# Attention, low-rank mixing and a feed-forward on one core: the feed-forward of batches 2 to 7 in tiles of 384 tokens instead of 288

## The chip, the core and the metric

The kernel runs on one NeuronCore of a Trainium2 chip. TensorE (PE) multiplies matrices into PSUM; VectorE (DVE), ScalarE (ACT) and GpSimd (POOL) do the element-wise work; SyncE (SP) issues the transfers. Each engine takes its instructions strictly in the order in which they were written into its queue. The metric is the device time of one execution in microseconds (us); lower is better. Differences under about 0.2% (2 us) are within what a measurement of this kernel can tell from no change.

## The reference

Eight batches, eight heads, 576 positions, 64 numbers per head. For each batch the kernel computes attention, mixes it over the positions with a matrix of rank 32, and puts a feed-forward of width 2048 behind it:

```python
q_d, k_d, v_d = means over groups of 4 positions          # 144 positions
out_up   = repeat(softmax(q_d k_d^T / 8) v_d, 4)           # coarse attention
out_local = softmax(masked q k^T / 8, |i - j| < 4) v       # local attention, 7 keys
x  = (out_up + out_local), heads side by side              # [576, 512] for a batch
u  = x + (x^T U V)^T                                       # U: 576x32, V: 32x576
out = u + relu(u w1) w2                                    # w1: 512x2048, w2: 2048x512
```

Everything is float32. The kernel splits each operand of the large products into a high and a low part and sums three products (high by high, high by low, low by high), so that TensorE's one-pass form of float32 keeps the accuracy.

## The kernel before

**Feed-forward.** The 4608 tokens (8 batches of 576) are cut into 16 tiles of 288, two for each batch. For a tile, `u` lies transposed in SBUF as `uH` and `uL`, four blocks of 128 channels each. The hidden width of 2048 is cut into 16 chunks of 128. A step is one tile and one chunk: `ffn1` (line 893) makes the chunk of the hidden layer in one PSUM bank with 12 matmuls (4 channel blocks by 3 products), ACT writes its relu as `hH`, DVE the rest as `hL`; three steps later `ffn2` (line 915) adds the chunk's part of the output to four PSUM banks with 12 matmuls (4 output blocks by 3 products). Each of these matmuls has 128 weight columns of its own and 288 moving columns, and each is preceded by its weight load. After the 16th chunk POOL adds `uH` and `uL` into an output buffer `o1`, DVE adds the PSUM bank, and SP stores it. There are 256 steps, 6144 matmuls.

**Attention.** The eight heads of a batch are done as four pairs. Pairs 0 to 3 (batch 0) take an early path at the start. The other 28, called late pairs here, go through this chain: scores on PE (lines 745 and 758), softmax of the coarse attention, its product with `v` (line 564), a store to memory (`up_s`, line 573) and a load in another layout (`ul`, line 817); the local attention in five pieces, in which POOL multiplies (`Pt`, line 829) and DVE sums (line 834); a store (`x_s`, line 836) and two loads, `xL` with positions across partitions (line 852) and `Y` in blocks of 32 (line 863). DVE transposes `Y` into `xT` (line 868); ACT rounds `xL` into `xH` (line 869), POOL takes the difference (line 870), PE multiplies both with `U` (line 878, "hu"), the result goes into `stk`, and PE multiplies it with `V` (line 715, "u"). DVE adds `xT`, and ACT and POOL write the pair's block of `uH` and `uL` for both tiles of the batch (lines 719 to 724). A tile's first step needs all four blocks.

**Buffers.** `uH` and `uL` have room for two tiles: the one in work and the next. `xT` has four places, one for each pair of a batch. `xL`, `xH` and `Y` have one place each, `Pt` three.

**What sets the order.** Nothing runs when it is defined. Every operation goes into a plan with a duration, a latency, a priority and the buffers it uses; `Plan.run` (line 94) plays the plan through on five model engines and then emits the instructions in the order of the start times that it found. On the chip this order is fixed for each engine. Attention operations of pair p have priorities of 10 p and a little more, feed-forward matmuls 1000 and more: a feed-forward step fills PE wherever no attention operation is ready in the model. `dma` (line 261) gives a transfer its model latency, with an addition `late` that grows with the priority.

Of the kernel before, what the change touches and what calls it, by code (L numbers as in the profile page):

```python
# [200 lines left out]
def attn_mix_ffn_kernel(ctx: ExitStack, tc, q, kp, vp, qT, kT, v, U, Ub, V, w1, w2, edge, band, eye, pool, vw, ident, outT):  # L201
# [507 lines left out]
    def u_tail(b, hp, stk, lt, xT, bank, prio):  # L709
        for t in range(NT):  # L710
            tsl = slice(t * TN, (t + 1) * TN)
            pu = bank("ps_u", 1 - t)

            def um(tsl=tsl, pu=pu):
                nc.tensor.matmul(pu()[:, :TN], lt(), Vst[:, tsl], start=True, stop=True)  # L715
# [6 lines left out]
            act(TN, lambda uH=uH, uf=uf: nc.scalar.activation(uH()[:, hp, :], uf(), AF.Copy),  # L722
                [ufk], [(uH, hp)], prio, 0.1)
            pool_tt(TN, lambda uH=uH, uL=uL, uf=uf: nc.gpsimd.tensor_tensor(  # L724
                out=uL()[:, hp, :], in0=uf(), in1=uH()[:, hp, :].bitcast(F32), op=ALU.subtract),
                [ufk, (uH, hp)], [(uL, hp)], prio)
# [114 lines left out]
    def u_of(b, t):
        if (b, t) not in u_bufs:
            u_bufs[(b, t)] = (buf(ffn, [128, NDC, TN], F32R, "uH", bufs=2), buf(ffn, [128, NDC, TN], F32R, "uL", bufs=2))
        return u_bufs[(b, t)]
# [211 lines left out]
```

## Time and profile before

| what | value |
|---|---|
| median of 3 runs | 1018.7 us (1018.46 to 1018.81) |
| profiled execution, its own time | 1018.72 us |
| span of that execution, first to last instruction | 1016.9 us, so 1.8 us lie outside it |
| mean granted TensorE clock | 0.991 of full speed |
| PE busy | 981.1 us (96%) |
| POOL, DVE, ACT busy | 578.6, 471.1, 387.5 us (57%, 46%, 38%) |
| mean busy share of the 16 DMA engines (kernel's own queue) | 46.2% |

A row that groups instructions gives the line of the kernel, the engine, the operation, what is written and read, the shapes and the count, then the time in which at least one of them ran, the mean of one in ns, the engine's idle time just before them, and what ended it. Matmuls overlap: one is shown as about 297 ns long, while the next starts after less than half of that, so for PE the distance from start to start tells more than the duration. In a table of windows the number behind an engine's busy time is the count of instructions that touch the window, and PEclk is the granted clock as a share of full speed.

### The profile page before, as it was taken

How to read it: one execution, taken by the hardware profiler on the slowest of the kernel's cores; microseconds unless marked ns; L12 is line 12 of the kernel's file. 1: busy time of each engine (PE TensorE's matmuls, PEld its weight loads, DVE VectorE, ACT ScalarE, POOL GpSimd, SP SyncE). 2: the span in 40 equal slices, each digit the busy share in tenths (PEclk: the TensorE clock that was granted, in tenths of full speed). 3: DMA queues.
4: the chain of work that ended last, by engine and by line, in shares of the span. 5: the costliest groups of instructions: out<-in, count | busy, mean ns of one | idle time of the engine just before them, and what ended most of it. 6: DMA issues, size and time to landing. Idle time of an engine off the chain costs nothing.

```text
span 1016.9 us, 26970 instructions
## 1 busy us (share of the span) xinstructions
PE 981.1 (96%) x10820; PEld 962.4 (95%) x10820; DVE 471.1 (46%) x945; ACT 387.5 (38%) x1239; POOL 578.6 (57%) x651
## 2 busy tenths in 40 slices
PE   5889899999999999999999999999999999999998
PEld 4679789989999999999999999999999999999998
DVE  5788864534544445454443445445443344221111
ACT  4866644433343342443443333333433232111110
POOL 6667897867565557675756657476675543211010
PEclk9979999999999999999999999999999999999999
DMA  9677955646364465564455553446555241000000
GB/s 262 196 233 210 278 132 125 169 100 148 81 148 106 120 134 138 119 142 106 106 144 123 139 122 92 114 101 159 132 130 122 65 99 53 8 6 19 6 20 24
DMA packets 222981, 120.23 MB, mean 118 GB/s; under 512 B 174772, under 2 KB 199176, under 8 KB 222856
## 3 DMA queue, kind: packets, MB, share of 16 engines
q1 hardware_dynamic: 222856, 118.51, 46.2%
q8 instruction: 85, 1.39, 0.6%
q14 instruction: 40, 0.33, 0.1%
HBM read 87.60 MB, written 30.86 MB: 116 GB/s over the span
## 4 chain that ended last, share of the span: by engine, by line
PE 87%; DMA 3%; POOL 3%; ACT 3%; DVE 2%; issue 1%; SPq 1%; POOLq 0%; ACTq 0%; DVEq 0%
PE ps_h L902 37%; PE acc L926 37%; PE ps_a L564 3%; PE ps_b L745 2%; PE ps_hu L878 2%; PE ps_t L551 1%; DMA vr<-in_v 1%; PE ps_b L758 1%; DMA gT<-in_kT 1%; POOL Pt L829 1%; PE ps_u L715 1%; POOL W L357 1%; PE ps_a L499 1%; DMA wr<-in_W 0%; DMA xL<-x_s 0%
## 5 line engine op out<-in xcount | busy, mean ns | idle before, releaser
L926 PE MATMUL acc<-hH,W 128*128 128x288 f32 x2048 | 463.1, 299 | 3.0 <-POOL W L357 3.0
L902 PE MATMUL ps_h<-uH,W 128*128 128x288 f32 x2048 | 455.5, 297 | 6.3 <-DVE hL L911 5.9
L902 PEld LDWEIGHTS ps_h<-uH,W 128*128 128x128 f32 x2048 | 345.6, 189 | 8.3 <-DVE hL L911 7.4
L926 PEld LDWEIGHTS acc<-hH,W 128*128 128x128 f32 x2048 | 344.3, 188 | 5.1 <-POOL W L357 4.1
L902 PE MATMUL ps_h<-uL,W 128*128 128x288 f32 x1024 | 304.0, 297 | 2.2 <-POOL uL L724 2.2
L911 DVE SCALAR_TENSOR_TENSOR hL<-ps_h,hH 128x288 fp32r<-128x288 f32 x256 | 116.7, 456 | 400.6 <-ACT hH L910 400.0
L926 PE MATMUL acc<-hL,W 128*128 128x288 f32 x1024 | 301.2, 294 | 0.0
L829 POOL TENSOR_TENSOR Pt<-vl,at 128x896 f32<-128x896 f32 (+1 forms) x140 | 242.5, 1808 | 56.4 <-DVE acc L834 49.9
L910 ACT ACTIVATE hH<-ps_h 128x288 fp32r<-128x288 f32 x256 | 105.1, 410 | 440.2 <-PE ps_h L902 440.1
L902 PEld LDWEIGHTS ps_h<-uL,W 128*128 128x128 f32 x1024 | 193.9, 189 | 2.4 <-POOL uL L724 2.4
L926 PEld LDWEIGHTS acc<-hL,W 128*128 128x128 f32 x1024 | 192.9, 188 | 0.0
L834 DVE TENSOR_REDUCE acc<-Pt 128x128 f32<-128x1024 f32 (+1 forms) x140 | 150.9, 1104 | 9.4 <-POOL Pt L829 4.8
L870 POOL TENSOR_TENSOR xL<-xL,xH 116x640 fp32r<-116x640 f32 x28 | 44.0, 1571 | 91.5 <-ACT xH L869 82.0
L724 POOL TENSOR_TENSOR uL<-xT,uH 128x288 fp32r<-128x288 f32 x64 | 50.2, 808 | 70.2 <-ACT uH L722 70.1
L937 POOL TENSOR_TENSOR o<-uH,uL 128x288 f32<-128x288 f32 x64 | 49.7, 811 | 55.1 <-DMA out_t<-o 55.1
L776 ACT ACTIVATE se<-ps_b 96x114 f32<-96x114 f32 x112 | 40.0, 357 | 57.1 <-PE ps_b L751 35.6
L823 ACT ACTIVATE Pt<-ul 128x128 f32<-128x128 f32 (+1 forms) x140 | 49.8, 442 | 21.6 <-DVE acc L834 17.6
L522 POOL TENSOR_TENSOR vr<-vr 72x256 f32<-72x256 f32 x56 | 41.4, 740 | 23.7 <-DMA vr<-in_v 23.7
L357 POOL TENSOR_TENSOR W<-c,W 128x512 fp32r<-128x512 f32 x32 | 41.3, 1292 | 13.1 <-ACT W L354 12.8
L537 ACT ACTIVATE E<-ps_b,nb 72x144 f32<-72x144 f32 x112 | 40.9, 373 | 0.6
L532 DVE TENSOR_REDUCE mx<-ps_b 72x2 f32<-72x288 f32 x56 | 23.1, 448 | 35.4 <-ACT se L776 32.9
L940 DVE TENSOR_TENSOR o<-acc,o 128x288 f32<-128x288 f32 x64 | 26.6, 452 | 24.3 <-PE acc L926 21.9
(134 smaller groups left out, 894.6 us busy)
## 6 DMA issues: line engine op xcount, KB each, us to landing
wr<-in_W SPq DMA_DIRECT2D x32, 512.0 KB
vl<-in_vp SPq DMA_DIRECT2D x56, 240.0 KB
vr<-in_v SPq DMA_DIRECT2D x64, 144.0 KB
out_t<-o SPq DMA_DIRECT2D x64, 144.0 KB
gT<-in_kT SPq DMA_DIRECT2D x28, 291.0 KB
gq<-in_qT SPq DMA_DIRECT2D x28, 288.0 KB
up_s<-od SPq DMA_DIRECT2D x112, 72.0 KB
ul<-up_s SPq DMA_DIRECT2D x28, 288.0 KB
```

The source lines that it names most:

```text
L357: pool_tt(1.0 * n, lambda: nc.gpsimd.tensor_tensor(out=lo_out(), in0=ta()[l0:], in1=hi_out()[l0:].bitcast(F32), op=ALU.subtract), [t, *own ...
L522: pool_tt(256, lambda x=x: nc.gpsimd.tensor_tensor(out=x()[:, :, 0:2, :], in0=x()[:, :, 0:2, :], in1=x()[:, :, 2:4, :], op=ALU.add), [x], ...
L724: pool_tt(TN, lambda uH=uH, uL=uL, uf=uf: nc.gpsimd.tensor_tensor(out=uL()[:, hp, :], in0=uf(), in1=uH()[:, hp, :].bitcast(F32), op=ALU.su ...
L823: act(n * D, lambda n=n, ps=ps, Pt=Pt: nc.scalar.activation(Pt()[:, :n, :, 7], ul()[:, ps, :], AF.Copy), [ul], [(Pt, 1)], prio, 0.16)
L829: nc.gpsimd.tensor_tensor(out=Pt()[:, :n, :, 0:7].rearrange("p s d o -> p o s d"), in0=win, in1=at()[:, ps, :].rearrange("p s o -> p o s") ...
L834: dve(8.5 * n * D, lambda n=n, ps=ps, Pt=Pt: nc.vector.tensor_reduce(out=acc()[:, ps, :], in_=Pt()[:, :n], axis=AX.X, op=ALU.add), [(Pt, 0 ...
L870: pool_tt(640, lambda: nc.gpsimd.tensor_tensor(out=xL(), in0=xL().bitcast(F32), in1=xH().bitcast(F32), op=ALU.subtract), [xL, xH], [xL], prio)
L902: nc.tensor.matmul(ps()[:, :TN], W1[fc]()[:, w, dc, :], u()[:, dc, :], start=(n == 0), stop=(n == 3 * NDC - 1))
L910: last_h[i] = act(TN, lambda: nc.scalar.activation(hH(), ps()[:, :TN], AF.Relu), [ps], [hH], FIRST, 0.05)
L911: dve(TN, lambda: nc.vector.scalar_tensor_tensor(hL(), ps()[:, :TN], 0.0, hH().bitcast(F32), op0=ALU.max, op1=ALU.subtract), [ps, hH], [hL ...
L926: nc.tensor.matmul(ac[e]()[:, :TN], W2[fc]()[:, w, es], hx(), start=(fc == 0 and n == 0), stop=(fc == NFC - 1 and n == 2))
L937: pool_tt(TN, lambda e=e, o1=o1: nc.gpsimd.tensor_tensor(out=o1()[:, :TN], in0=uH()[:, e, :].bitcast(F32), in1=uL()[:, e, :].bitcast(F32), ...
```

## The change

- **Tiles.** Batches 0 and 1 keep their four tiles of 288 tokens. The 3456 tokens of batches 2 to 7 are cut into nine tiles of 384, across the borders of batches: of each three tiles the middle one holds 192 tokens of one batch and 192 of the next. A matmul of these tiles has 384 moving columns. There are 13 tiles, 208 steps and 4992 feed-forward matmuls, 3456 of them 384 wide.
- **The last product of a pair** ("u", now line 720) is cut at the borders of tiles: for batches 2 to 7 into 384 and 192 columns in place of 288 and 288.
- **Room.** The fourth channel block of the wide `uH` and `uL` lies in a place of its own (`u3`); `Y` and `xH` share one place; `Pt` has two places instead of three; the attention weights `at` are written over `ms`, which gets two places; the scratch of the weight conversion and the output buffers share one tile, cut into three and four.
- **The model behind the order.** A transfer's added latency falls from 1.5 or 2.0 us (priority 50 to 79) and 3.0 or 4.0 us (80 and more) to 0.25 and 0.5 us. A matmul's model duration follows its width. `U` is loaded between the tenth and eleventh weight chunks instead of after the last.

```diff
-    TN = 288
+    TN, TW = 288, 384
+    NB = 2
-    PH, PF = 1.587, 0.398
+    PE_N = lambda n, k: k * (n / 2400.0 + 0.0125)
+    UC = 10
...
     def dma(fn, r, w, prio, kb=295.0, issue=0.47, lat=1.3, after=()):
-        late = (3.0 if r else 4.0) * (0.5 * (prio >= 50) + 0.5 * (prio >= 80))
+        late = 0.25 * (prio >= 50) + 0.25 * (prio >= 80)
...
+    conv = buf(ffn, [128, 3 * CN], I32, "conv", "cT:c", 1)
...
     def u_tail(b, hp, stk, lt, xT, bank, prio):
-        for t in range(NT):
-            tsl = slice(t * TN, (t + 1) * TN)
+        for t, (ti, tsl, us) in enumerate(segs[b]):
+            n = tsl.stop - tsl.start
...
-                nc.tensor.matmul(pu()[:, :TN], lt(), Vst[:, tsl], start=True, stop=True)
-            op(PE, 0.14, um, [(stk, 0), (stk, 1), (stk, 2), "V0H", "V1H", "V0L", "V1L"], [pu], prio)
+                nc.tensor.matmul(pu()[:, :n], lt(), Vst[:, tsl], start=True, stop=True)
+            op(PE, PE_N(n, 1), um, [(stk, 0), (stk, 1), (stk, 2), "V0H", "V1H", "V0L", "V1L"], [pu], prio)
...
-        ms, mx = lb([128, NPOS, 7], "ms"), lb([128, NPOS], "lmx")
+        ms, mx = lb([128, NPOS, 7], "ms", bufs=2), lb([128, NPOS], "lmx")
...
-        at = lb([128, NPOS, 7], "at", bufs=2)
+        at = ms
...
-            Pt = buf(loc, [128, 2, D, 8], F32, "Pt", "Pt", 3)
+            Pt = buf(loc, [128, 2, D, 8], F32, "Pt", "Pt", 2)
...
+    tiles, segs = [], {}
+    for g0 in (*range(0, NB * S, TN), *range(NB * S, B * S, TW)):
+        n = TN if g0 < NB * S else TW
+        for b in range(g0 // S, (g0 + n - 1) // S + 1):
+            lo, hi = max(g0, b * S), min(g0 + n, (b + 1) * S)
+            segs.setdefault(b, []).append((len(tiles), slice(lo - b * S, hi - b * S), slice(lo - g0, hi - g0)))
+        tiles.append((g0, n))
...
+    class Half:
+        def __init__(self, ti, name):
+            n = tiles[ti][1]
+            if n == TN:
+                w = buf(ffn, [128, NDC, TN], F32R, name, bufs=2)
+                self.parts = [(w, dc) for dc in range(NDC)]
+            else:
+                w = buf(ffn, [128, NDC - 1, TW], F32R, name, bufs=2)
+                x = buf(loc, [128, TW], F32R, "u3", "u3", 4)
+                self.parts = [(w, dc) for dc in range(NDC - 1)] + [(x, None)]
...
-        xH = buf(mix, [MP, 2, MJ, D], F32R, "xH")
+        xH = buf(mix, [MP, 2, MJ, D], F32R, "xH", "xH:x")
...
-        Y = buf(mix, [128, S // 32, 32], F32, "Y")
+        Y = buf(mix, [128, S // 32, 32], F32, "Y", "xH:y")
...
-                    nc.tensor.matmul(ps()[:, :TN], W1[fc]()[:, w, dc, :], u()[:, dc, :],
+                    nc.tensor.matmul(ps()[:, :tn], W1[fc]()[:, w, dc, :], u.ap(dc),
...
-                    nc.tensor.matmul(ac[e]()[:, :TN], W2[fc]()[:, w, es], hx(),
+                    nc.tensor.matmul(ac[e]()[:, :tn], W2[fc]()[:, w, es], hx()[:, :tn],
...
-    steps = [(b, t, fc) for b in range(B) for t in range(NT) for fc in range(NFC)]
+    steps = [(ti, fc) for ti in range(len(tiles)) for fc in range(NFC)]
```

**Where the order changes: SP, the last pair of batch 1.** Its `x_s` store and the loads behind it, at the door of tile 2 (the first of batch 1). Before:

```order
L836 DMA x_s<-acc 128x576
L573 DMA up_s<-od 288x1x64 x4
L581 DMA gq<-in_qT 128x576
L581 DMA gT<-in_kT 128x582
L784 DMA s_s<-se 32x3x38 x3
L784 DMA s_s<-se 32x9x38
L852 DMA xL<-x_s 112x2x320
L855 DMA xL<-x_s 4x2x320
L863 DMA Y<-x_s 32x18x32 x4
```

Now:

```order
L841 DMA x_s<-acc 128x576
L525 DMA vr<-in_v 72x2x256
L578 DMA up_s<-od 288x1x64 x4
L887 DMA xL<-x_s 112x2x320
L890 DMA xL<-x_s 4x2x320
L898 DMA Y<-x_s 32x18x32 x4
```

The loads of `gq` and `gT` and the four stores of scores (`s_s`) of a later pair no longer stand between the store of `x_s` and the loads of it; one load of `vr` does.

**POOL at the same door.** From the difference `xL` of that pair to its `uL` of the two tiles of batch 1, the last blocks that tile 2 waits for. Before:

```order
L870 TENSOR_TENSOR xL<-xL,xH 116x640
L829 TENSOR_TENSOR Pt<-vl,at 128x7x128
L522 TENSOR_TENSOR vr<-vr 72x2x128
L428 TENSOR_TENSOR gh<-gq 128x288
L524 TENSOR_TENSOR vs<-vr 72x128
L430 TENSOR_TENSOR smq<-gh 128x144
L829 TENSOR_TENSOR Pt<-vl,at 128x7x128
L724 TENSOR_TENSOR uL<-xT,uH 128x288 x2
```

Now:

```order
L905 TENSOR_TENSOR xL<-xL,xH 116x640
L834 TENSOR_TENSOR Pt<-vl,ms 128x7x128 x2
L834 TENSOR_TENSOR Pt<-vl,ms 128x7x64
L729 TENSOR_TENSOR uL<-xT,uH 128x288 x2
```

Four short operations on `vr`, `gh`, `vs` and `smq` moved behind `uL`, and the local attention's last, half-size `Pt` moved ahead of it.

**PE between "hu" and "u" of a pair.** The second pair of batch 6 before, and the first pair of batch 5 now:

```order
L878 MATMUL ps_hu<-xL,Ust 64x128 x5
L564 MATMUL ps_a<-vs,E 72x64 x8
L902 MATMUL ps_h<-uH,W_7_1150 128x288
L902 MATMUL ps_h<-uL,W_7_1150 128x288
L902 MATMUL ps_h<-uH,W_7_1150 128x288 x2
L902 MATMUL ps_h<-uL,W_7_1150 128x288
L902 MATMUL ps_h<-uH,W_7_1150 128x288 x2
L902 MATMUL ps_h<-uL,W_7_1150 128x288
L902 MATMUL ps_h<-uH,W_7_1150 128x288 x2
L902 MATMUL ps_h<-uL,W_7_1150 128x288
L902 MATMUL ps_h<-uH,W_7_1150 128x288
L715 MATMUL ps_u<-Vst,stk 128x288 x2
```

```order
L913 MATMUL ps_hu<-xL,Ust 64x128 x5
L963 MATMUL acc_8185<-hH,W_15_2319 128x384
L963 MATMUL acc_8185<-hL,W_15_2319 128x384
L963 MATMUL acc_8185<-hH,W_15_2319 128x384
L963 MATMUL acc_8201<-hH,W_15_2319 128x384
L963 MATMUL acc_8201<-hL,W_15_2319 128x384
L963 MATMUL acc_8201<-hH,W_15_2319 128x384
L963 MATMUL acc_8209<-hH,W_15_2319 128x384
L963 MATMUL acc_8209<-hL,W_15_2319 128x384
L963 MATMUL acc_8209<-hH,W_15_2319 128x384
L720 MATMUL ps_u<-Vst,stk 128x192
L720 MATMUL ps_u<-Vst,stk 128x384
```

The feed-forward rows are wide now, and u has two unequal parts. Between the "hu" of one pair and that of the next stood 96 to 282 feed-forward matmuls before. Now the four pairs of batch 5 stand close together, with 72, 57 and 72 matmuls between them, those of batch 6 with 78, 66 and 60, and those of batch 7 with 66, 72 and 72; 447 or more separate these three clusters from what is ahead of batches 5 and 7, 183 from batch 6.

More of the change, by code (lines that the diff above doesn't have):

```diff
@@ L304, in attn_mix_ffn_kernel @@
     kept = {}
-    count = {"y": 0}
+    count = {"y": 0, "c": 0}
+    conv = buf(ffn, [128, 3 * CN], I32, "conv", "cT:c", 1)
     def ring(shape, name, n=2, eng=None):
@@ L332, in convert @@
     def convert(raw, pp, n, hi_out, lo_out, a, wkey, name, prio, own_bank=False, l0=0):
-        t = buf(ffn, [128, CN], I32, name, "cT:" + name, 3)
+        ck = count["c"] % 3
+        count["c"] += 1
+        t = (conv, ck)
         if own_bank:
@@ L837, in local_attn, with ap, key, keys @@
             [(acc, p) for p in range(0, NPOS, 2)], [(x_s, 0), (x_s, 1)], prio)
-    u_bufs = {}
[L841 to L844, printed above, removed]
+    tiles, segs = [], {}
[5 more added lines that the diff above has]
+        tiles.append((g0, n))
+    u_bufs = {}
+    class Half:
[8 more added lines that the diff above has]
+                self.parts = [(w, dc) for dc in range(NDC - 1)] + [(x, None)]
+            self.ti, self.n = ti, n
+        def ap(self, dc, c=slice(None)):
+            x, k = self.parts[dc]
+            a = x()[:, 0:self.n] if k is None else x()[:, k, :]
+            return a[:, c]
+        def key(self, dc, b):
+            return (self.parts[dc][0], dc, b)
+        def keys(self, dc):
+            return [self.key(dc, b) for b in range(B) for t, _, _ in segs[b] if t == self.ti]
+    def u_of(ti):
+        if ti not in u_bufs:
+            u_bufs[ti] = (Half(ti, "uH"), Half(ti, "uL"))
+        return u_bufs[ti]
     def mix_part(b, hp, x_s, prio):
         xL = buf(mix, [MP, 2, MJ, D], F32R, "xL")
-        xH = buf(mix, [MP, 2, MJ, D], F32R, "xH")
+        xH = buf(mix, [MP, 2, MJ, D], F32R, "xH", "xH:x")
         def load():
@@ L893, in ffn1 @@
     def ffn1(s, i):
-        b, t, fc = s
-        uH, uL = u_of(b, t)
+        ti, fc = s
+        tn = tiles[ti][1]
+        uH, uL = u_of(ti)
         ps = psum(ps_h, "ps_h", f"h{i % 2 * (i >= H1):d}:f", 1)
@@ L930, in ffn2 @@
         if fc == NFC - 1:
[L931 removed]
+            uH, uL = u_of(ti)
+            o = buf(ffn, [128, 3 * CN], F32, "o1", "cT:o", 1)
             for e in range(NDC):
[L933 to L942 removed]
+                o1 = lambda e=e: o()[:, e * TW:e * TW + tn]
+                pool_tt(tn, lambda e=e, o1=o1: nc.gpsimd.tensor_tensor(
+                    out=o1(), in0=uH.ap(e).bitcast(F32), in1=uL.ap(e).bitcast(F32), op=ALU.add),
+                    uH.keys(e) + uL.keys(e), [(o, e)], FIRST, after=[last_h[i - 1]])
+                dve(tn, lambda e=e, o1=o1: nc.vector.tensor_tensor(
+                    out=o1(), in0=ac[e]()[:, :tn], in1=o1(), op=ALU.add),
+                    [ac[e], (o, e)], [(o, e)], FIRST)
@@ L943, in ffn2 @@
                 dma(lambda e=e, o1=o1: nc.sync.dma_start(
-                    out=outT[e * 128:(e + 1) * 128, b * S + t * TN:b * S + (t + 1) * TN], in_=o1()[:, :TN]),
-                    [o1], [], FIRST, 150, lat=0.4)
-    steps = [(b, t, fc) for b in range(B) for t in range(NT) for fc in range(NFC)]
+                    out=outT[e * 128:(e + 1) * 128, g0:g0 + tn], in_=o1()),
+                    [(o, e)], [], FIRST, tn / 1.92, lat=0.4)
+    steps = [(ti, fc) for ti in range(len(tiles)) for fc in range(NFC)]
@@ L979, in attn_mix_ffn_kernel @@
         p.gate.append(late)
-    load_u(36)
     edge_sb = buf(loc, [128, QL + 2 * KL], BF16, "edge")
@@ L983, in attn_mix_ffn_kernel @@
     attention(1)
+    opener = {segs[b][0][0] * NFC: b + 1 for b in range(1, B - 1)}
     for i in range(len(steps) + LAG):
         if i < len(steps):
-            b, t, fc = steps[i]
-            if t == 0 and fc == 0 and b > 0 and b + 1 < B:
-                attention(b + 1)
+            if i in opener:
+                attention(opener[i])
             ffn1(steps[i], i)
```

58 lines of the change are left out of this document (25 added, 33 removed).

## The prediction

> **What bounds the kernel now.** I read the page's first part, then the time cut into stretches, then the groups of instructions.
>
> ```profile
> span 1016.9 us, 26970 instructions
> PE 981.1 (96%) x10820; PEld 962.4 (95%) x10820; DVE 471.1 (46%) x945; ACT 387.5 (38%) x1239; POOL 578.6 (57%) x651
> ```
>
> PE is busy 96% of the span, the next engine 57%. A table of windows (length, then busy time of PE and count, granted clock, DMA share, GB/s; PE alone) says where the missing 36 us are:
>
> ```profile
> 0.00:240.00 240.00, 207.97 (x2777) 0.96 0.69 188
> 240.00:1000.00 760.00, 759.82 (x7948) 1.00 0.41 98
> 880.00:1000.00 120.00, 120.00 (x906) 1.00 0.03 11
> 1000.00:1016.90 16.90, 13.28 (x100) 0.98 0.11 36
> 207.20:209.20 2.00, 2.00 (x10) 0.50 0.00 0
> ```
>
> 32.0 us of idleness lie before 240 us, 3.6 in the tail, and between them PE stands still for 0.2 us. There no other engine and no transfer sets the time: the end is the sum of PE's own spacings. What fills PE is the feed-forward:
>
> ```profile
> L926 PE MATMUL acc<-hH,W 128*128 128x288 f32 x2048 | 463.1, 299 | 3.0 <-POOL W L357 3.0
> L902 PE MATMUL ps_h<-uH,W 128*128 128x288 f32 x2048 | 455.5, 297 | 6.3 <-DVE hL L911 5.9
> L902 PE MATMUL ps_h<-uL,W 128*128 128x288 f32 x1024 | 304.0, 297 | 2.2 <-POOL uL L724 2.2
> L926 PE MATMUL acc<-hL,W 128*128 128x288 f32 x1024 | 301.2, 294 | 0.0
> ```
>
> The counts add up to 6144. Their mean of 297 ns is no price, since they overlap: the distance from start to start is. Between 880 and 1000 us only feed-forward is left; of the 906 matmuls that touch this window about two hang in from before it, so 120 us / 904 = **132.8 ns** each at 288 columns.
>
> **The spacing at 384 columns.** No such matmul stands in this trace, so the price has to be split into a part that grows with the columns and one that doesn't. At the door of tile 2 the granted clock is 0.50 (last window row). Its matmuls stand exactly 0.24 us apart (timeline of PE: start, length):
>
> ```profile
> 208.60 0.45 PE L902 MATMUL ps_h<-uL,W 128*128 128x288 f32 x1
> 208.84 0.45 PE L902 MATMUL ps_h<-uH,W 128*128 128x288 f32 x1
> ```
>
> At half clock 288 columns take 240 ns with nothing on top, 0.833 ns a column; at the full clock that is 120 ns, and 132.8 − 120 = 12.8 ns are a fixed part. If it stays, 384 columns take 160 + 12.8 = **172.8 ns**. The Trainium skill, "TensorE: Matmul & The Clock Gate", section "What's actually happening", says that the clock is halved after an idle window of some 3.4 us; the 0.50 after the waits of the door, listed further down, agrees. Two bounds. Above: everything grows with the width, 132.8 × 384/288 = 177.1. Below: the nearest other shape, the hu matmuls, 128 columns wide:
>
> ```profile
> 313.45 0.47 PE L878 MATMUL ps_hu<-xH,Ust 116*64 116x128 f32 x5
> 313.76 0.47 PE L878 MATMUL ps_hu<-xL,Ust 116*64 116x128 f32 x5
> 314.06 0.35 PE L926 MATMUL acc<-hH,W 128*128 128x288 f32 x1
> ```
>
> Ten of them fill 0.61 us, 61.0 each, of which 128 × 0.4167 = 53.3 are columns: a fixed part of 7.7 ns, which would make 167.7. These load 64 weight columns where the feed-forward loads 128, so a fixed part that goes with the weights stays at 12.8; I take 172.8, since the feed-forward keeps its weight shape and only the moving side widens.
>
> Tiles 0 to 3 keep their 1536 matmuls. The other 12 of 16 tiles have 4608; the change makes 3456 of them (9 tiles of 384), over the same columns in sum. Before: 4608 × 0.1328 = 611.9 us. After: 3456 × 0.1728 = 597.2. **Term: −14.7 us**; by the bounds 0.0 (177.1) and −32.3 (167.7).
>
> A rule that speaks for much more: the Trainium skill, same page, section "Wait — 56ns, not 53.3ns?", gives N/2.4 + 2.5 ns from start to start. At 288 that is 122.5, and the trace has 132.8, so it disagrees here; by it 384 columns would take 162.5 and the term would be −50.3. That is the third rival.
>
> **The rest of the change.** *The last product "u"*: 384 and 192 columns instead of 288 and 288, as many columns and instructions: nothing. *ACT's and DVE's passes on a step* get a third wider, but there are fewer, and both engines are below half busy: nothing, unless they come late for ffn2, which stands three steps behind. *U between weight chunks*: SP's order there is the same, and hu first runs at 129.5 us, far behind it: nothing. *`Pt` with two places, `at` over `ms`*: they tighten the local attention on POOL, which is 57% busy; covered while PE has feed-forward to do.
>
> *The door of tile 2.* At 202 us PE runs out of feed-forward and waits for the last pair of batch 1 (timeline of PE; in brackets the idle time and its releaser):
>
> ```profile
> 200.00 0.51 PE L878 MATMUL ps_hu<-xL,Ust 116*64 116x128 f32 x5 [0.36 <-POOL xL L870]
> 201.55 0.50 PE L715 MATMUL ps_u<-Vst,stk 128*128 128x288 f32 x2 [1.04 <-DVE stk L883]
> 203.69 0.40 PE L902 MATMUL ps_h<-uH,W 128*128 128x288 f32 x1 [0.44 <-ACT uH L722]
> 206.26 0.40 PE L902 MATMUL ps_h<-uL,W 128*128 128x288 f32 x1 [2.17 <-POOL uL L724]
> ```
>
> That is 4.0 us, and about 13 matmuls at half clock behind it cost 13 × 0.107 = 1.4 more: 5.4 in all. The chain of this pair before the door, on SP, ACT and POOL:
>
> ```profile
> 190.13 0.47 SPq L581 DMA_DIRECT2D gq<-in_qT  x1
> 191.16 1.79 SPq L784 DMA_DIRECT2D s_s<-se  x4
> 193.00 0.46 SPq L852 DMA_DIRECT2D xL<-x_s  x1
> 197.56 0.74 ACT L869 ACTIVATE xH<-xL 116x640 fp32r<-116x640 f32 x1 [1.49 <-DMA xL<-x_s]
> 199.90 1.87 POOL L829 TENSOR_TENSOR Pt<-vl,at 128x896 f32<-128x896 f32 x1
> 203.72 1.83 POOL L829 TENSOR_TENSOR Pt<-vl,at 128x896 f32<-128x896 f32 x1
> 205.41 1.56 POOL L724 TENSOR_TENSOR uL<-xT,uH 128x288 fp32r<-128x288 f32 x2
> 206.91 1.04 POOL L829 TENSOR_TENSOR Pt<-vl,at 128x448 f32<-128x448 f32 x1
> ```
>
> SP's two loads and four stores (193.00 − 190.13 = 2.87 us) leave the way of `xL`; one `vr` load, about as long as the one `gq` issue of 0.47, enters: 2.4 us earlier, of which ACT waited 1.49 for the transfer. On POOL the difference and `uL` had 5.5 us between them (199.90 to 205.41); now two whole `Pt` and a half one stand there, 1.87 + 1.83 + 1.04 = 4.7: 0.8 us less, but uL waits for uH in any case. The gain has a ceiling of 5.4. The other way, tile 1's own matmuls may run out sooner or POOL be late for its new order: a microsecond lost. I take **−2.0**, the 1.49 and something over half of the 0.8 (range −5.4 to +1).
>
> *One place for `Y` and `xH`.* `xH` may be written only after DVE has read `Y`, and the next pair's `Y` be loaded only after hu has read `xH`. So the pairs of a batch hang in a loop: load, transpose, round, difference, hu. Its links as another pair shows them:
>
> ```profile
> 437.85 0.45 SPq L852 DMA_DIRECT2D xL<-x_s  x1
> 438.75 2.61 SPq L863 DMA_DIRECT2D Y<-x_s  x4
> 444.62 0.78 DVE L868 STREAM_TRANSPOSE xT<-Y 128x576 f32<-128x576 f32 x1 [1.80 <-DMA Y<-x_s]
> 443.56 0.73 ACT L869 ACTIVATE xH<-xL 116x640 fp32r<-116x640 f32 x1
> 445.81 1.58 POOL L870 TENSOR_TENSOR xL<-xL,xH 116x640 fp32r<-116x640 f32 x1
> 447.72 2.05 POOL L829 TENSOR_TENSOR Pt<-vl,at 128x896 f32<-128x896 f32 x1
> ```
>
> From the issue of `xL` to `Y` landed 444.62 − 437.85 = 6.77; transpose 0.78, `xH` 0.73, difference 1.58, hu 0.61; with five hand-overs of about 0.1 each (an estimate) 11.0 us. The time there is for it is the feed-forward between one hu and the next: the nine counts of batches 5 to 7 (72, 57, 72, 78, 66, 60, 66, 72, 72), times 0.1728, and 0.9 for the hu and u in between: 10.8 to 14.4 us, 114.4 in sum; elsewhere the distance is several times that. At 11.0 only the count of 57 is short, by 0.2. If a whole `Pt` of 2.05 stands ahead of the difference each time, the loop is 13.1 and four are short, by some 5.8 in all. PE would wait there, strictly in order, and the feed-forward behind it; on SP the stores of `o` and the next pair's `ul` and `gq` are queued behind a `Y` that waits, and have the rest of the round to land. I take the middle, **+3.0** (0.2 to 5.8).
>
> *Shorter model latencies.* Loads that the model thinks landed are used sooner. The waits before (total, times, longest):
>
> ```profile
> ACT xH L869 <- DMA xL<-x_s: 4.1, 3, 1.5
> ACT Pt L823 <- DMA ul<-up_s: 3.4, 4, 1.5
> ```
>
> Behind such a wait on ACT stands the next step's `hH`; ffn2 wants it three steps later, some 12 us in the wide tiles. None reached PE between 240 and 1000 us, where PE stood 0.2 us. I take nothing for them, and up to 0.3 us for each of 24 pairs as the upper end.
>
> *Tail.* The last `o` addition on DVE (452 ns at 288 columns, 1.65 us for the four pieces together) grows by a third: **+0.2** for the piece that nothing covers.
>
> **Sum.** −14.7 − 2.0 + 3.0 + 0.2 = −13.5. The profiled execution took 1018.72 (span 1016.9 and 1.8 outside it), within 0.1 of the median of 1018.7: **1005.2 us**, a span of 1003.4.
>
> **The rivals.**
>
> 1. *The spacing grows with the width.* All 12.8 ns scale, 177.1 ns. For it: nothing but one full-speed width with 128 weight columns; against it, at half clock there is no remainder at all, so it isn't columns. Then 1018.72 − 0.0 − 2.0 + 3.0 + 0.2 = 1019.9, no change. Chance 0.08, a third of it beyond the 0.2% (2 us) that a measurement can tell.
> 2. *A smaller fixed part.* 167.7 ns as in hu: 1018.72 − 32.3 + 1.2 = 987.6. For it the hu rows; against it the weights of half the width there. Chance 0.09.
> 3. *The fixed part vanishes behind a wide matmul*, because the weight load then has more cover: 160 ns, 3456 × 0.160 = 553.0, −58.9, so 961.0. Against it: PEld is busy 95% and PE 96%, so neither is seen to wait for the other, and no row names the load as what the 12.8 ns wait for. Chance 0.03. By the page's 2.5 ns it would be 969.6.
> 4. *Slower: the shared place of `Y` and `xH`.* If in each round of the loop an issue of four `up_s` stores, which takes SP
>
> ```profile
> 186.64 3.37 SPq L573 DMA_DIRECT2D up_s<-od  x4
> ```
>
>    3.37 us, stands ahead on SP and a `Pt` ahead on POOL, a round is 11.0 + 3.4 + 2.0 = 16.4 us; nine rounds are 147.6, against 114.4 there is, 33.2 us of waits instead of 3.0: 1035.4. It decides from a round of 14.5 us (9 × 14.5 − 114.4 = 16.1, the gain and my 3.0 together). Against it: SP can issue such stores while it waits for the hu ahead, and need not do so in each of nine rounds. Chance 0.04.
> 5. *Slower: transfers are late, as the old latencies assumed.* If each of the 24 pairs of batches 2 to 7 passes on a wait of 4.1/3 = 1.37 us, PE loses 32.9: 1038.1. It decides from 0.56 a pair. Against it: the three steps of lead. Chance 0.04.
>
> **Numbers.** Forecast 0.72, its own range 998 to 1011 (door and loop by their bounds, the spacing by 1 ns either way, 3.5 us). The rivals take 0.08, 0.09, 0.03, 0.04, 0.04. From 994 to 1020 the range holds the forecast and rival 1, 0.80. Faster: 0.72 + 0.09 + 0.03 = 0.84; no change 0.05; slower 0.03 + 0.04 + 0.04 = 0.11.
>
> **What would show it.** The spacing is read from a late window of pure feed-forward: 40 us should hold some 231 matmuls; 226 is rival 1, 238 rival 2, 250 rival 3. The door: PE's waits for `stk`, uH and uL near 195 to 207 us should sum to 2 rather than 4 us. The loop: PE waiting at hu (now line 913) for `xL` or `xH` in batches 5 to 7, together up to 6 us; 30 is rival 4. Late transfers would show as PE waiting at ffn2 for `hH` or `hL`. The forecast is wrong if PE has more than some 10 us of idleness after 240 us, or if the fixed part isn't fixed.

## The result, and the profile after

The changed kernel takes **1022.25 us** (median of 8 runs, 1020.23 to 1025.26) against 1018.54 for the kernel before in the same session: a ratio of **1.0041, 95% interval 1.0027 to 1.0054**. It is slower by 3.7 us; 1005.2 was forecast, and the value lies above the range of 994 to 1020. Its runs also scatter over 5 us, those of the kernel before over 2.5. The profiled execution took 1021.17 us. Its page:

```profile
span 1019.4 us, 24571 instructions
PE 976.5 (96%) x9668; PEld 952.2 (93%) x9668; DVE 462.4 (45%) x885; ACT 387.0 (38%) x1191; POOL 573.2 (56%) x639
...
PE 71%; POOL 8%; DMA 7%; DVE 4%; issue 3%; ACT 3%; SPq 3%; DVEq 0%; POOLq 0%; ACTq 0%
```

The last row is the chain that ended last. Before, PE had 87% of it, POOL and DMA 3% each; now there are stretches in which the end hangs on transfers and on POOL. The windows of PE alone (length, busy time, count, granted clock, DMA share, GB/s):

```profile
0.00:240.00 240.00, 206.51 (x2772) 0.94 0.69 187
240.00:1000.00 760.00, 754.14 (x6828) 1.00 0.41 98
900.00:1000.00 100.00, 100.00 (x577) 1.00 0.03 9
```

In the quiet end 100 us hold 575 matmuls of 384 columns (two of the 577 hang in): **173.9 ns** each, 1.1 more than forecast. So 3456 × 0.1739 = 601.0 us, and the spacings save 611.9 − 601.0 = 10.9 us. They do save; something else gives back 13.5. PE stands still for 5.9 us between 240 and 1000 us, where it was 0.2, and the clock has sunk from 0.96 to 0.94 ahead of 240.

To find the place I priced every matmul at its undisturbed spacing (132.8 and 173.9 ns for the feed-forward; small shapes at their mean in the kernel before after 240 us), summed the prices up to each moment and took the sum from the time on the clock. The difference is PE's lost time: waiting, half clock and changes between kinds of work. Its growth by stretch, in us:

| kernel | 0–100 | 100–140 | 140–200 | 200–240 | 240–320 | 320–440 | 440–640 | 640–end | sum |
|---|---|---|---|---|---|---|---|---|---|
| before | 44.5 | 9.1 | 1.5 | 6.6 | 0.9 | 2.3 | 2.8 | 2.7 | 70.4 |
| changed | 44.6 | 11.8 | 1.0 | 7.6 | 1.2 | 8.8 | 5.5 | 3.6 | 83.9 |

−10.9 + 13.5 = 2.6, against 2.45 between the two profiled executions. Most of the loss lies in 320 to 440 us (+6.5), then 440 to 640 (+2.7) and 100 to 140 (+2.7). Each row comes from one profiled execution. Where the clock is halved for 3.4 us, that alone can cost 1.7 us, and it doesn't fall alike in every execution (see the door of tile 2), so a difference of 2 us in a single cell says little.

Between 100 and 140 us PE isn't idle for longer than before; what differs is the granted clock (before, then changed):

```profile
100.00:140.00 40.00, 33.50 (x343) 1.00 0.77 219
100.00:140.00 40.00, 33.78 (x318) 0.87 0.82 213
```

0.13 of 40 us are 5.2 us of clock; the stretch lost 2.7 us more than before, so half clock can account for all of it. Why the clock was halved there is not shown.

**The door of tile 2.** A door is the moment at which the last blocks of a tile are written and its first step may start. This one became cheaper, in part for the reason given (timeline of PE):

```profile
205.10 0.50 PE L720 MATMUL ps_u<-Vst,stk 128*128 128x288 f32 x2 [2.38 <-DVE stk L918]
207.10 0.40 PE L938 MATMUL ps_h<-uH,W 128*128 128x288 f32 x1 [0.30 <-ACT uH L727]
208.09 0.40 PE L938 MATMUL ps_h<-uL,W 128*128 128x288 f32 x1 [0.59 <-POOL uL L729]
```

The waits sum to 3.3 us instead of 4.0, where 2 had been forecast, and no half clock stands behind them: 4.3 us lost between 200 and 220 us instead of 6.4. That the half clock stayed away isn't the change's doing alone. In a later run of the kernel before, with its operands moved by 32 bytes and the same planned order, it stayed away too, although the waits there sum to 4.5 us (before, that run, changed; the number behind the count is the granted clock):

```profile
200.00:220.00 20.00, 16.35 (x204) 0.91 0.42 111
200.00:220.00 20.00, 16.74 (x221) 1.00 0.48 111
200.00:220.00 20.00, 16.72 (x229) 1.00 0.64 159
```

So 0.7 us of the gain is shorter waits; part of the rest is luck. And 20 us later a new wait stands, and it shows the kind (ACT, DVE and PE, in this order):

```profile
227.99 0.72 ACT L828 ACTIVATE Pt<-ul 128x128 f32<-128x128 f32 x2 [2.36 <-DMA ul<-up_s]
228.53 1.22 DVE L839 TENSOR_REDUCE acc<-Pt 128x128 f32<-128x1024 f32 x1 [2.59 <-ACT Pt L828]
229.67 0.81 DVE L724 TENSOR_TENSOR xT<-ps_u,xT 128x384 f32<-128x384 f32 x2
230.27 1.25 PE L569 MATMUL ps_a<-vs,E 72*72 72x64 f32 x16 [1.31 <-DVE xT L724]
```

A load of `ul` lands late, ACT waits 2.36 us in front of `Pt`, DVE 2.59 behind ACT; DVE's `xT` of another pair is queued behind that, and PE waits for it. Then the clock is halved for 3.4 us (granted 0.83 in 230 to 240 us). The waits for transfers over the whole kernel (total, times, longest):

```profile
POOL vr L527 <- DMA vr<-in_v: 33.0, 13, 6.6
ACT Pt L828 <- DMA ul<-up_s: 30.9, 15, 4.3
DVE xT L903 <- DMA Y<-x_s: 18.0, 7, 5.7
POOL Pt L834 <- DMA vl<-in_vp: 15.9, 6, 3.8
POOL gh L433 <- DMA gq<-in_qT: 9.0, 7, 2.0
```

In the kernel before they were 23.7, 3.4, 2.2, 5.7 and 1.2 us. The longest of them there, which the prediction didn't list:

```profile
POOL vr L522 <- DMA vr<-in_v: 23.7, 9, 9.3
```

### The profile page after: what moved, and what is told of

Its sections match the earlier page's. It is cut to its first block, busy times and chain, and to the rows that moved or that the text cites. A ratio compares the mean times of both kernels' runs of the same rounds, so it can differ in the third digit from the quotient of the medians.

```text
span 1019.4 us, 24571 instructions
## 1 busy us (share of the span) xinstructions
PE 976.5 (96%) x9668; PEld 952.2 (93%) x9668; DVE 462.4 (45%) x885; ACT 387.0 (38%) x1191; POOL 573.2 (56%) x639
## 4 chain that ended last, share of the span: by engine, by line
PE 71%; POOL 8%; DMA 7%; DVE 4%; issue 3%; ACT 3%; SPq 3%; DVEq 0%; POOLq 0%; ACTq 0%
PE acc L963 31%; PE ps_h L938 30%; POOL Pt L834 4%; PE ps_a L569 2%; PE ps_b L750 2%; DMA ul<-up_s 2%; DVE acc L839 1%; DMA vr<-in_v 1%; SPq L578 1%; PE ps_hu L913 1%; DMA wr<-in_W 1%; PE ps_b L763 1%; PE ps_t L556 1%; DMA vl<-in_vp 1%; PE ps_u L720 1%
## 5 line engine op out<-in xcount | busy, mean ns | idle before, releaser
L963 PE MATMUL acc<-hH,W 128*128 128x384 f32 (+1 forms) x1664 | 446.0, 329 | 3.1 <-POOL W L362 1.7
L938 PE MATMUL ps_h<-uH,W 128*128 128x384 f32 (+1 forms) x1376 | 360.2, 323 | 6.0 <-DVE hL L947 5.6
L963 PE MATMUL acc<-hL,W 128*128 128x384 f32 (+1 forms) x832 | 269.7, 324 | 0.0
L834 POOL TENSOR_TENSOR Pt<-vl,ms 128x896 f32<-128x896 f32 (+1 forms) x140 | 239.7, 1788 | 42.7 <-DVE acc L839 25.3
L947 DVE SCALAR_TENSOR_TENSOR hL<-ps_h,hH 128x384 fp32r<-128x384 f32 (+1 forms) x208 | 108.8, 523 | 327.0 <-ACT hH L946 326.1
L938 PEld LDWEIGHTS ps_h<-uH,W 128*128 128x128 f32 x1376 | 246.1, 190 | 7.7 <-DVE hL L947 6.8
L938 PE MATMUL ps_h<-uL,W 128*128 128x384 f32 (+1 forms) x688 | 221.5, 322 | 1.1 <-POOL uL L729 1.1
L946 ACT ACTIVATE hH<-ps_h 128x384 fp32r<-128x384 f32 (+1 forms) x208 | 97.4, 468 | 325.4 <-PE ps_h L938 321.6
L938 PE MATMUL ps_h<-u,W 128*128 128x384 f32 x432 | 99.6, 339 | 0.0
L938 PEld LDWEIGHTS ps_h<-u,W 128*128 128x128 f32 x432 | 77.4, 187 | 0.0
```

The source lines that it names most:

```text
L834: nc.gpsimd.tensor_tensor(out=Pt()[:, :n, :, 0:7].rearrange("p s d o -> p o s d"), in0=win, in1=at()[:, ps, :].rearrange("p s o -> p o s") ...
L938: nc.tensor.matmul(ps()[:, :tn], W1[fc]()[:, w, dc, :], u.ap(dc), start=(n == 0), stop=(n == 3 * NDC - 1))
L946: last_h[i] = act(tn, lambda: nc.scalar.activation(hH()[:, :tn], ps()[:, :tn], AF.Relu), [ps], [hH], FIRST, 0.05)
L947: dve(tn, lambda: nc.vector.scalar_tensor_tensor(hL()[:, :tn], ps()[:, :tn], 0.0, hH()[:, :tn].bitcast(F32), op0=ALU.max, op1=ALU.subtract ...
L963: nc.tensor.matmul(ac[e]()[:, :tn], W2[fc]()[:, w, es], hx()[:, :tn], start=(fc == 0 and n == 0), stop=(fc == NFC - 1 and n == 2))
```

## The experiments

Two theories stood at first. **L**: the short latencies put loads too close to their users. **S**: the shared and fewer places make the chains tight. The first runs brought up a third, **D**, on the dates at which a batch is due.

### Latency and places, one at a time

**The changed kernel with the old latencies:**

```diff
-        late = 0.25 * (prio >= 50) + 0.25 * (prio >= 80)
+        late = (3.0 if r else 4.0) * (0.5 * (prio >= 50) + 0.5 * (prio >= 80))
```

> The changed kernel with the old added latencies (1.5 or 2.0 us, and 3.0 or 4.0 us) in the model behind its order; tiles and places as changed. Theory L (the short latencies put loads so close to their users that ACT, DVE and POOL wait for transfers, and PE with them): ACT's waits for ul fall from 30.9 us to under 10, DVE's for Y from 18.0 to under 6, PE's idleness after 240 us from 5.9 to under 1.5, and the time to 1010 to 1014 us. Theory S (the shared and fewer places make the chains tight whatever the model believes): the waits for transfers may fall, but PE's idleness stays at 5 or more and the time at 1019 to 1024.

Measured: 1028.65 us, ratio 1.0103 (1.0078 to 1.0128). Both theories miss: the waits for `ul` and `Y` do fall, yet it is the slowest of all.

```profile
ACT Pt L828 <- DMA ul<-up_s: 6.8, 6, 2.1
DVE xT L903 <- DMA Y<-x_s: 3.9, 6, 1.0
```

PE's timeline shows why:

```profile
413.87 0.80 PE L913 MATMUL ps_hu<-xH,Ust 116*64 116x128 f32 x5 [2.93 <-ACT xH L904]
415.49 0.80 PE L913 MATMUL ps_hu<-xL,Ust 116*64 116x128 f32 x5 [0.82 <-POOL xL L905]
417.91 0.87 PE L720 MATMUL ps_u<-Vst,stk 128*128 128x192 f32 x2 [1.62 <-DVE stk L918]
```

This is a door: hu, u and then the first matmul of tile 5, nothing in between. PE has no feed-forward left, as at tile 2, and half clock follows; 320 to 440 us lose 11.7 us instead of 2.3. **Theory D:** tile 5 lies across the border of batches 2 and 3, so it needs all of batch 3's attention one tile after tile 4 opened. In the changed kernel tile 4 starts at 330.0 us and tile 5 at 414.4, 84 us later; before, the doors of batches 2 and 3 were 322.3 and 443.3, 121 us apart. Batches 4 and 6 get more time in return and don't need it (their last u is 81 and 95 us early in the changed kernel). The other odd batches, those whose first half lies in a tile across a border, are as late in this run: the last u of batches 5 and 7 ends at 657.4 and 890.1 us, and their tiles 8 and 11 start at 659.4 and 890.0. In the changed kernel itself no such door waits (batch 3's last u ends at 403.5); there the scattered waits cost instead.

**The kernel before with the short latencies alone:**

```diff
-        late = (3.0 if r else 4.0) * (0.5 * (prio >= 50) + 0.5 * (prio >= 80))
+        late = 0.25 * (prio >= 50) + 0.25 * (prio >= 80)
```

> The kernel before with only the short added latencies (0.25 and 0.5 us); tiles of 288 and all places as before. Theory L: waits for transfers on ACT, DVE and POOL grow as in the changed kernel (ACT for ul from 3.4 to over 20 us), PE stands still for some us after 240 us, and the time is 1022 to 1030 us. Theory S: waits for transfers grow but PE is covered; 1017 to 1020 us.

Measured: 1021.77 us, 1.0030 (1.0010 to 1.0050). As L has it in kind, 0.2 us below its range of 1022 to 1030:

```profile
POOL vr L522 <- DMA vr<-in_v: 75.9, 28, 7.3
DVE xT L868 <- DMA Y<-x_s: 30.6, 13, 5.9
ACT Pt L823 <- DMA ul<-up_s: 22.9, 14, 3.9
```

**The kernel before with `Y` and `xH` in one place:**

```diff
-        xH = buf(mix, [MP, 2, MJ, D], F32R, "xH")
+        xH = buf(mix, [MP, 2, MJ, D], F32R, "xH", "xH:x")
-        Y = buf(mix, [128, S // 32, 32], F32, "Y")
+        Y = buf(mix, [128, S // 32, 32], F32, "Y", "xH:y")
```

> The kernel before with only Y and xH in one place; tiles, latencies and the other places as before. Theory L: the planner keeps the four pairs of a batch 96 matmuls or more apart, PE is covered: 1017 to 1020 us. Theory S: PE waits at hu or u, 1022 to 1030 us.

Measured: 1017.37 us, 0.9995 (0.9977 to 1.0013): nothing.

**The kernel before with two places for `Pt` and `at` over `ms`** (the edits are those of the change):

> The kernel before with only two places for Pt, and the attention weights written over ms, which gets two places. Theory D: covered, 1017 to 1020 us. Theory S: 1021 to 1028 us.

Measured: 1019.25 us, 1.0004 (0.9983 to 1.0025): nothing in sum.

**All of the change but the wide tiles and the latencies** (`NB = 8`, old `late`):

> All of the changed kernel but its wide tiles and its latencies: 16 tiles of 288, u cut in 288 and 288, the shared and fewer places, U between the weight chunks, matmul durations in the model by width, the old latencies. Theory D: no border, no early door; only what the weight loading costs between 100 and 140 us (1.4 to 2.8 us in four kernels): 1018 to 1021 us. Theory S: 1024 us or more.

Measured: 1017.30 us, 0.9996 (0.9978 to 1.0013). S has fallen: the places, U's place and the model's matmul durations together cost nothing on the old tiles. From this kernel to that of the first run (the old latencies in both) nothing differs but the tiles, with the cut of u and the place of their fourth block, and the ratio goes from 0.9996 to 1.0103: the wide tiles by themselves are 10.9 us slower, though their spacings save 10.9.

### Does the wait move with the border?

**Wide tiles for batches 4 to 7 only, old latencies:**

```diff
-    NB = 2
+    NB = 4
...
```

> The changed kernel with tiles of 288 for batches 0 to 3 and 384 for batches 4 to 7 only, and the old added latencies; shared and fewer places as changed. Theory D (deadlines: tile 5 across the border needs batch 3 one tile after tile 4, 84 us later where two tiles of 288 left 121, and the attention of batch 3 isn't ready): with batches 2 and 3 back on their old dates nothing waits between 240 and 560 us; 3072 x 0.1328 - 2304 x 0.174 = 7.1 us fewer spacings, some 2.5 us lost between 100 and 140 us as in the two kernels with the same weight loading: 1012 to 1016 us. Theory S (the shared and fewer places, or the wide tiles themselves): PE still loses 8 to 10 us beside the spacings after 240 us: 1019 to 1026.

Measured: 1023.60 us, 1.0048 (1.0031 to 1.0066). The time is in S's range, the place is D's. From 320 to 640 us this kernel loses no more than the one before (1.9 and 2.8 us, table below). Then the first odd batch behind a border is due, batch 5 at tile 9:

```profile
647.90 0.52 PE L913 MATMUL ps_hu<-xH,Ust 116*64 116x128 f32 x5 [2.17 <-ACT xH L904]
649.52 0.52 PE L913 MATMUL ps_hu<-xL,Ust 116*64 116x128 f32 x5 [1.11 <-POOL xL L905]
651.94 0.87 PE L720 MATMUL ps_u<-Vst,stk 128*128 128x192 f32 x2 [1.90 <-DVE stk L918]
652.61 0.52 PE L938 MATMUL ps_h<-uH,W 128*128 128x384 f32 x1
652.93 0.52 PE L938 MATMUL ps_h<-uL,W 128*128 128x384 f32 x1
```

The same three waits, now 234 us later; the last two rows stand 0.32 us apart, half clock at 384 columns. 8.8 us are lost between 640 and 680 us, 1.2 at the next such door (tile 12). My forecast of 1012 to 1016 had left out that batches 5 and 7 come to such doors too. Tiles 8 and 9 start 90 us apart (562.9 and 652.6), and the pairs of batch 5 end their u at 569.8, 600.7, 632.0 and 652.8: the last one opens the door. Moving the border moved the wait: that is what D says, and it is shown for the old latencies.

**The same tiles with the short latencies:**

> The same tiles (288 for batches 0 to 3, 384 for 4 to 7) with the short added latencies. Theory D with the short latencies as a cost of their own (3.5 us on the kernel before): 1015 to 1019 us, above the same tiles with the old latencies. If the short latencies are what tiles across borders need, it is as fast as that or faster.

Measured: 1025.94 us, 1.0072 (1.0050 to 1.0094), above both expectations. No door waits across a border now (batch 5 is 40 us early), but the scattered waits cost more. Two costs stand against each other: long latencies make odd batches late, short ones make engines wait for transfers.

**Long latencies up to batch 4, short ones after it** (on these tiles):

```diff
-        late = 0.25 * (prio >= 50) + 0.25 * (prio >= 80)
+        late = ((3.0 if r else 4.0) if prio < 200 else 0.5) * (0.5 * (prio >= 50) + 0.5 * (prio >= 80))
...
```

> Tiles of 288 for batches 0 to 3 and 384 for 4 to 7, as in the two runs before, with the old added latencies for pairs 0 to 19 (batches 0 to 4) and the short ones for pairs 20 to 27 and on (batches 5 to 7), whose doors across borders come early. Theory D: neither the scattered waits that the short latencies cost ahead of 600 us nor the waits at the doors of tiles 9 and 12 (8.9 and 1.2 us with the old latencies): 7.1 us of spacings saved, 1 to 3 us lost early and late: 1012 to 1016 us, faster than both kernels. If the short latencies cost as much in the late batches, or the doors wait all the same: 1018 to 1024 us.

Measured: 1019.87 us, 1.0023 (1.0007 to 1.0040), above the 1012 to 1016 of theory D. No door across a border waits, but one scattered wait lies where the short latencies begin (POOL, then PE):

```profile
547.31 0.73 POOL L527 TENSOR_TENSOR vr<-vr 72x256 f32<-72x256 f32 x1 [3.09 <-DMA vr<-in_v]
554.47 1.22 PE L569 MATMUL ps_a<-vs,E 72*72 72x64 f32 x8 [2.43 <-POOL vs L529]
```

POOL waits 3.09 us for an input, PE 2.43 for what POOL makes of it, and with the half clock behind it 5.7 us are lost.

### Which transfers

`vr`, `vl`, `gq` and `gT` read inputs. They wait for nothing but a free place, and a long latency in the model only makes the plan put other work between the load and its user. `up_s`, `ul`, `s_s`, `sc`, `x_s`, `xL` and `Y` follow one another in a pair's chain; a long latency there makes the pair later.

**Tiles of `NB = 4`; 0.5 us only for the chain of batches 5 to 7:**

```diff
...
+        late = ((0.5 if prio >= 200 else 3.0) if r else 4.0) * (0.5 * (prio >= 50) + 0.5 * (prio >= 80))
...
```

> Tiles of 288 for batches 0 to 3 and 384 for 4 to 7; added latencies as before for all loads of inputs (4.0 us: vr, vl, gq, gT) and for every transfer of batches 0 to 4; only the transfers that follow a store or an operation in the chain of a pair (up_s, ul, s_s, sc, x_s, xL, Y) of batches 5 to 7 get 0.5 us. The run before this one lost 5.7 us at 554 us, where PE waited 2.4 us for vs, behind a late vr load. If late loads of inputs are what the short latencies cost there: that loss is gone, 7.1 us of spacings stay saved, 1013 to 1017 us. If the transfers in the chain cost as much: 1018 to 1023.

Measured: 1016.52 us, 0.9988 (0.9976 to 1.0000), 0.35% below the run before it, as forecast for late loads of inputs.

**The changed kernel, inputs at 4.0 us, the chain at 0.5:**

```diff
+        late = (0.5 if r else 4.0) * (0.5 * (prio >= 50) + 0.5 * (prio >= 80))
```

> The changed kernel (384 from batch 2 on) with the old 4.0 us for loads of inputs and 0.5 us for the transfers in the chain of a pair. If its scattered waits between 340 and 440 us come from inputs that land late, PE's loss between 320 and 440 us falls from 8.9 to 5 us or less, what is left at the door of tile 5: 1015 to 1019 us. If they come from ul, Y and the door itself: 1020 to 1025.

Measured: 1017.89 us, 1.0003 (0.9989 to 1.0017); 320 to 440 us lose 3.0 us instead of 8.8. Nothing but the model latency of four loads of inputs differs from the changed kernel, and 0.38% or 3.9 us are back.

```profile
ACT Pt L828 <- DMA ul<-up_s: 16.7, 11, 5.4
DVE xT L903 <- DMA Y<-x_s: 12.7, 14, 2.9
POOL vr L527 <- DMA vr<-in_v: 10.0, 7, 2.4
```

POOL's waits for `vr` fall from 33.0 to 10.0, and those for `ul` and `Y` fall too, though their own latency stayed short. The largest loss that remains after 140 us is the door of tile 2: 10.1 us from 200 to 240, of which half clock can account for 3.4 (granted 0.83 in 200 to 220 us).

**The same, with the chain of batch 1 at its old 1.5 us:**

```diff
+        late = ((0.5 if prio >= 80 else 3.0) if r else 4.0) * (0.5 * (prio >= 50) + 0.5 * (prio >= 80))
```

> The changed kernel (384 from batch 2 on) with the old added latencies for batch 1 and for all loads of inputs, and 0.5 us for the transfers in the chain of a pair from batch 2 on. If the 10.2 us lost at the door of tile 2 in the run before come from batch 1's short latencies, that loss is back at 6 to 7 us and the time 2 to 4 us lower than there: 1013 to 1016 us. If not: 1017 to 1020.

Measured: **1014.35 us, 0.9956 (0.9940 to 0.9973)**, faster than both kernels: all of batches 2 to 7 in wide tiles.

The door of tile 2 loses 4.1 us in 200 to 240 (6.6 before, 7.6 changed, 10.1 in the run above). PE stands idle there for 2.6 us instead of 6.6: these 4.0 us are what batch 1's short chain had cost. The other 2 go with the half clock, which stayed away here (granted 1.00 in 200 to 220 us). At the door of tile 5 PE still waits:

```profile
409.41 0.53 PE L720 MATMUL ps_u<-Vst,stk 128*128 128x192 f32 x2 [2.52 <-DVE stk L918]
412.41 0.61 PE L938 MATMUL ps_h<-u,W 128*128 128x384 f32 x2 [0.71 <-POOL u L729]
```

Lost time by stretch in eight of the kernels above, one execution each, as in the first table (its first column and that of 140 to 200 us, in which they differ by 3 us at most, are left out):

| kernel | 100–140 | 200–240 | 240–320 | 320–440 | 440–640 | 640–end | sum | ratio |
|---|---|---|---|---|---|---|---|---|
| before | 9.1 | 6.6 | 0.9 | 2.3 | 2.8 | 2.7 | 70.4 | 1 |
| changed | 11.8 | 7.6 | 1.2 | 8.8 | 5.5 | 3.6 | 83.9 | 1.0041 |
| changed, old latencies | 11.2 | 6.2 | 1.6 | 11.7 | 4.1 | 9.9 | 91.7 | 1.0103 |
| before, short latencies | 10.8 | 4.2 | 1.7 | 3.7 | 5.1 | 3.3 | 75.0 | 1.0030 |
| wide from batch 4, old | 10.3 | 6.5 | 2.0 | 1.9 | 2.8 | 13.0 | 82.5 | 1.0048 |
| wide from batch 4, chain of 5 to 7 short | 10.2 | 6.2 | 1.8 | 1.7 | 5.1 | 4.0 | 76.7 | 0.9988 |
| wide from batch 2, chain short | 10.3 | 10.1 | 2.7 | 3.0 | 4.0 | 4.3 | 80.4 | 1.0003 |
| wide from batch 2, chain short from batch 2 | 11.0 | 4.1 | 1.7 | 7.0 | 4.4 | 3.4 | 76.4 | 0.9956 |

**U next to last among the weight chunks**, on top of the fastest kernel:

```diff
-    UC = 10
+    UC = 18
```

> The same with U loaded and converted next to last among the weight chunks, not between the tenth and eleventh. If U's conversion ahead of weight chunks makes PE wait for weights between 100 and 140 us (1.4 to 2.8 us more than before in six kernels), PE's loss there falls to that of the kernel before and the time by 1 to 3 us more: 1011 to 1015 us. If the shared scratch or chance does it: no gain between 100 and 140.

Measured: 1014.81 us, 0.9960 (0.9945 to 0.9975): no gain, and not as forecast. 100 to 140 us lose 16.7 us instead of 11.0, since the first late pair now waits itself:

```profile
129.98 0.48 PE L913 MATMUL ps_hu<-xH,Ust 116*64 116x128 f32 x5 [1.46 <-POOL Pt L834]
131.55 0.80 PE L913 MATMUL ps_hu<-xL,Ust 116*64 116x128 f32 x5 [1.09 <-POOL xL L905]
134.31 0.82 PE L720 MATMUL ps_u<-Vst,stk 128*128 128x288 f32 x2 [1.96 <-DVE stk L918]
```

The door of tile 2, with that order, loses 0.6 us instead of 4.1, so the sum hardly moves. Since other waits came into the stretch, this run doesn't tell whether U's place costs anything. Nor is the changed weight loading shown to be the cause of the 1 to 3 us that most kernels with it lose more between 100 and 140 us: the kernel before with the short latencies alone has the old loading and loses 1.7 more there too. The shared scratch wasn't tried by itself.

### The price of a matmul

**The kernel before, its operands moved by 32 bytes:**

```diff
-    warm = const.tile([128, 1], F32, name="warm")
+    warm = const.tile([128, 16], F32, name="warm")
...
```

> The kernel before with a first constant of 64 bytes a partition in place of 4, which moves every later tile by 32 bytes; the moving operands of the feed-forward, at 32 modulo 64 before, then start at a multiple of 64. The order is the same. If a part of the 12.8 ns beyond the columns is read lines that an operand touches in excess (a run of 1152 bytes touches 19 lines of 64 bytes at an offset of 32, and 18 at none), the spacing of 288 columns falls from 132.8 to about 126 ns and the time by some 40 us to about 980. If the fixed part has nothing to do with the address, the spacing stays at 132.8 and the time at 1018.5.

Measured: 1017.99 us, 0.9999 (0.9986 to 1.0011); the quiet window holds the same 906 matmuls. Moving the operands by 32 bytes changes nothing.

**Several widths in one kernel:**

```diff
+    NARROW = {(11, 0): 320, (11, 1): 256, (12, 0): 192}
+    cols = lambda ti, fc: NARROW.get((ti, fc // 8), TW) if fc and ti >= 11 else tiles[ti][1]
...
```

> The changed kernel with the moving side of the last two tiles cut: after its first chunk tile 11 uses 320 columns in chunks 1 to 7 and 256 in chunks 8 to 15, tile 12 uses 192 in chunks 1 to 7 and 384 after; the columns left out make the output of these tiles wrong. Spacings in the quiet end: with a fixed part of 12.8 ns 320 columns give 146.1, 256 give 119.5, 192 give 92.8; with a part that grows with the columns (132.8 at 288, 174.0 at 384 are 0.4292 ns a column and 9.2 ns) 146.5, 119.1 and 91.6. The time falls by some 20 us for the columns left out.

Measured: 999.76 us, in one run; the columns left out save time here, so only the spacings say something. PE's timeline, for each width two rows that are 10, 12 and 12 matmuls apart:

```profile
897.76 0.46 PE L941 MATMUL ps_h<-uH,W 128*128 128x320 f32 x2
899.23 0.31 PE L967 MATMUL acc<-hH,W 128*128 128x320 f32 x1
...
925.05 0.28 PE L967 MATMUL acc<-hH,W 128*128 128x256 f32 x1
926.49 0.28 PE L941 MATMUL ps_h<-uH,W 128*128 128x256 f32 x1
...
948.86 0.27 PE L967 MATMUL acc<-hH,W 128*128 128x192 f32 x1
950.19 0.28 PE L941 MATMUL ps_h<-uH,W 128*128 128x192 f32 x1
```

1.47/10 = 147 ns at 320 columns, 1.44/12 = 120.0 at 256, 1.33/12 = 110.8 at 192. Above the columns' 0.4167 ns each these leave 13.7, 13.3 and 30.8 ns, beside 12.8 at 288 and 13.9 at 384. From 256 to 384 columns the part beyond them is nearly fixed; at 192 something else sets the distance.

## Why the prediction was wrong

- **Spacing, −14.7 us.** The mechanism held, the size not quite: 173.9 ns and −10.9. The fixed part at 384 is 13.9, not 12.8 ns. Rivals 1 to 3 are out. The rule of the Trainium skill, "TensorE: Matmul & The Clock Gate", section "Wait — 56ns, not 53.3ns?", would have 162.5; the trace disagrees at every width, by 10 to 12 ns from 256 up.
- **Door of tile 2, −2.0 us.** −2.1 between 200 and 220 us, near the forecast, but partly by luck: the waits fell by 0.7, not by 2, and the rest is mostly the half clock, which stayed away in a run with the old order too. The wait at 230 us, 20 us behind the door, gave back 3.1 (stretch of 220 to 240), so the term as a whole came out at +1.0.
- **One place for `Y` and `xH`, +3.0 us.** Wrong: 0 (0.9995 alone). PE waits nowhere at hu in batches 5 to 7 of the changed kernel.
- **Shorter latencies, nothing.** This is the first of two steps that failed. It argued that the waits in the kernel before never reached PE. But that trace shows waits in an order that had been planned with long latencies; it says nothing of one planned with short ones. The row for `ul` went from 3.4 to 30.9 us, and the latencies alone cost the kernel before 0.3%. The two kinds of transfer stand against each other: on the wide tiles the short latencies of the chain gain about 10 us (1.0103 to 1.0003 by them alone), and those of the input loads cost 3.9 (1.0003 to 1.0041). Rival 5 has the mechanism of the second, with a chance of 0.04. It priced 24 pairs at 1.37 us each; after 200 us the changed kernel loses 11.4 us more than the one before, or 0.48 a pair, and not all of that is late transfers. I also counted only ACT's waits; inputs that POOL waits for (`vr`, `vl`) weren't in the list, though `vr` with 23.7 us was the longest wait for a transfer in that trace, and they were what the run with inputs at 4.0 us gave back.
- **What no term had: the dates.** This is the second step that failed, and the larger one. The sum gave the wide tiles no cost but the loop of `Y` and `xH`, and took PE to be covered by feed-forward everywhere else. I counted the feed-forward matmuls between the pairs of batches 5 to 7, where there was room, and not the distance between the doors of batches 2 and 3, where it fell from 121 to 84 us. With the old latencies that stretch costs 9.4 us (11.7 instead of 2.3), and the wide tiles are 10.9 us slower in place of faster; the short latencies avoid the door and pay elsewhere. So leaving the latencies alone would not have saved the forecast. The two halves of the change aren't independent, and pricing them one by one could not give the sum.
- **Tail, +0.2**, is too small to be told.

In sum: −10.9 for the spacings, +2.8 ahead of 140 us, −0.5 from 140 to 200, +1.0 at the door and behind it, +10.4 after 240 us, 2.8 with roundings, against 2.45 between the two profiled executions. Shown by runs is that the short latencies of input loads cost the changed kernel 3.9 us, and that with long latencies the early doors cost it more (the border moved, and the wait with it). Why the changed kernel with long latencies for its input loads still loses 10 us more than the one before, how the +2.8 comes about (half clock has a part in it), and why the fastest kernel waits at the door of tile 5 again, is not.

## What to carry to other kernels

Where a planner fixes an order, its latencies for loads that can be issued early and for transfers that follow one another in a chain are two different knobs: too short for the first and engines stand in queue order behind data that hasn't come, too long for the second and a whole chain is late. When tiles are cut across the borders of the work that feeds them, list the date at which each piece is due before counting what the wider tiles save. And a trace bounds a wait only for the order that it shows.
